# Lead-in of an attention block with a gated Mish layer: one row turned on TensorE, eight maxima moved behind the first step

## The chip, the cores and the metric

One core of a Trainium2 chip. The metric is device time in microseconds of one execution, the median of three runs. Engines: PE (TensorE) multiplies, PEld is its weight load, DVE is VectorE, ACT ScalarE, POOL GpSimd, SP SyncE, which here only issues DMAs. All matrices are 32-bit floats.

## The reference

```python
xn = layernorm(x)                       # x: 2048 x 512
q, k, v = xn @ wq, xn @ wk, xn @ wv     # 32 query heads of 16, one key and one value head of 16
p = softmax(q_h @ k.T / 4)              # per head, 2048 x 2048
s = concat_h(p @ v) @ wo
g = silu(mish(xn @ w1 + b1) @ w2)       # 1792 hidden columns
return x + s * g
```

## The kernel before, in words

Queries come in 4 chunks of 512 rows. With 32 heads that makes 128 head-chunk pairs; four of them are a **unit** `v` (32 units), held in a tile `qt` of 128 partitions: two halves `a` of 64 partitions, and two column planes `p`. Per half a query has 16 high rows, 16 high rows again, 16 low rows and, in rows 48 and 49, its negated row maximum in two parts; `ks` holds the keys' high and low parts with ones below, so that one matmul over 64 rows gives the score less the maximum.

A **step** is one block of 128 keys for one unit; there are 512. In a step TensorE computes four score tiles **E** (line 1056), ScalarE takes their exponentials into `pt` (line 1058), and two steps later eight **PV** matmuls (line 1143) add value-weighted sums, a column of ones giving the softmax's divisor. The maxima of a unit must be known before its first E: for each 128 queries and 512 keys, TensorE computes a score tile **M** (line 1078) and VectorE reduces it to a maximum (line 1082). A unit has 64 such maxima, four in each step on average, worked about a unit ahead (`LEAD = 20` steps). What is left of TensorE goes to **X**, the projections `xps` (query, Mish and output layers), of which a chunk of up to eight stands in each step: the function `waves` pairs a half matmul of X on 64 rows of the array with an E or M on the other 64. A large X group ends with its bank being copied out.

Ahead of step 0 is the **lead-in**. There x is normalized, transposed (line 303) and projected to keys and values in four chunks (line 341, bank `kp`). ScalarE writes the keys' high part (line 346) and copies the value part (line 355), VectorE writes the low part (line 238); TensorE turns the values (line 360) and VectorE copies them into `vaug` (line 363). The four use the same bank `kp`/`vp`, so a chunk's projection follows the copy of the chunk before. Lead-in work is ordered by a small planner: each task has an engine, an estimated duration, the tasks it depends on, and a priority; at each turn the earliest is written out. Maxima are not tasks: `m_ready` says when the next pair (one of each half, both halves side by side) can go, in the order `MSEQ`, by the arrival of query rows (`qready`), of the key chunk (`kready`) and by free PSUM banks (three for M). X is filled in where TensorE would be idle. A list written by the planner fixes the order of each engine's instructions; the hardware then only waits.

The first unit's query rows are split by ScalarE (high, line 703) and VectorE (low) and moved by DMAs on SP's queue (line 721). When 68 maxima are there, all 64 of unit 0 among them, `c_rows` reduces them on VectorE to a row (lines 1104 to 1109), turns it in blocks of 32x32 (line 1114), and eight DMAs put the blocks into rows 48 and 49 of `qt` (line 1122). Maxima of unit 1 go on. The lead-in ends when the planner holds the row for moved and each half has `2 * LEAD` = 40 maxima, 80 in all; step 0 follows, with four maxima in each step from then on. In later units the row is made in the same way.

Of the kernel before, what the change touches and what calls it, by code (L numbers as in the profile page):

```python
# [32 lines left out]
NU = 8 * NC  # L33
LEAD = 20
NWARM = 24
E0 = 74
# [90 lines left out]
def block_kernel(ctx: ExitStack, tc: tile.TileContext, x, wq, wk, wv, wo, w1, b1, w2, out):  # L127
# [234 lines left out]
    def v_out(c):  # L362
        dve.tensor_copy(vaug[:, 4 * c:4 * c + 4, 0:DH], vp_of[c][:, :, 16:32])

# [330 lines left out]
    def q_group(c, b):  # L695
        it = item("wq", ("q", b), wq[:, P * b:P * (b + 1)].rearrange("(t p) n -> p t n", p=P))

        def post(ps):
# [12 lines left out]
            for k in range(2):  # L711
                v = 8 * c + 2 * b + k

                def dmas(v=v, k=k, parts=((0, 0), (0, 1), (1, 0), (1, 1))):
                    q = qt_of[v] = qts[v % 3]
                    for p, a in parts:
                        o = 64 * a
                        r = 64 * k + 16 * (2 * p + a)
                        for d, src in ((o, qh), (o + 16, qh), (o + 32, ql)):
                            sp_at(0.63)  # L720
                            sp.dma_start(f(q[d:d + 16, p]), f(src[r:r + 16]))  # L721
                if first:
                    lead["qdma"](lambda ps, dmas=dmas: dmas(parts=[(p, a) for p in ps for a in range(2)]))
                else:
                    for n in range(4):
                        at(16 * v - LEAD - 9 + 2 * n, lambda dmas=dmas, n=n: dmas(parts=(divmod(n, 2),)))

# [361 lines left out]

    def m_sides(h, n):  # L1090

        ahead = m_next[h] - m_next[1 - h]
        lo = max((4 - MLAG - ahead + 1) // 2, 4 - (32 * NU - m_next[1 - h]))
        hi = min((4 + MLAG - ahead) // 2, 32 * NU - m_next[h])
        return max(min(n, hi), lo)

    def c_rows(v):

        mp = sb.tile([P, 2, 3, 8], F32R, tag="mp", name=f"mp{v}", bufs=2)
        mx = f(mp[:, :, 0])  # L1100
# [15 lines left out]
        def move():  # L1116
            q, cr = qt_of[v], w["cr"]
            for a in range(1, -1, -1):
                r = 64 * a + 48
                for b in range(4):  # L1120
                    sp_at(0.68)
                    sp.dma_start(f(q[r:r + 2]).rearrange("o p (t b n) -> b o (p t) n", b=4, n=32)[b],
                                 cr[32 * b + 16 * a:32 * b + 16 * a + 16])
        return reduce, parts, turn, move

# [157 lines left out]

    def q_low(fn):
        lead["qlow"] = task("DVE", 0.69, fn, at=T["ACT"] + 0.7)

    def q_dma(fn):
        v = len(qready)
        qready[v] = None

        def move(p):
            fn(ps=(p,))
            qready[v] = (qready[v] or ()) + (now[0] + 6 * 0.63 + 2.0,)
        for p in range(2):
            task("SP", 6 * 0.63, lambda p=p: move(p), [lead["qlow"]], prio=1 + p + 2 * v)

# [25 lines left out]
    for c in range(A_LO // 4, NC):  # L1322
        sums = [task("ACT", 0.8, lambda t=t: stats_a(t, 0), at=xat[t], prio=2.8) for t in range(4 * c, 4 * c + 4)]
        means = task("ACT", 0.22, lambda c=c: means_a(slice(4 * c, 4 * c + 4)), sums, prio=2.8)
        st += [task("ACT", 0.8, lambda t=t: stats_a(t, 1), [means], prio=2.8) for t in range(4 * c, 4 * c + 4)]
    kv_done = None
    for c0, c1 in ((0, 1), (1, 2), (2, 3), (3, 4)):
        z = slice(4 * c0, 4 * c1)
# [8 lines left out]
        for c in range(c0, c1):  # L1337
# [47 lines left out]
            vc = task("ACT", 0.59, lambda c=c: v_copy(c), [kp], lat=0.7)  # L1385
            bank("v", 1, k0, [kl, vc])
            vtr = task("PE", 0.5, lambda c=c: v_transpose(c), [vc])
            vo = task("DVE", 0.22, lambda c=c: v_out(c), [vtr])
            bank("v", 1, vtr, [vo])

# [5 lines left out]
    def m_ready(t):  # L1396
        if min(m_next) >= 2 * LEAD or rows and rows[-1].end is None:
            return None
# [5 lines left out]
    def best(eng):  # L1404
        found = None
        for k in plan[eng]:
            s = k.start(T[eng])
            if s is not None:
                rank = max(s, T[eng] + 0.1) + WAIT_US * k.prio
                if found is None or rank < found[2]:  # L1410
                    found = (s, k, rank)
        return found

    begun = [0]
# [4 lines left out]
    while True:  # L1419
# [12 lines left out]
        if m is not None and b and b[0] < T["PE"] + 0.2 and T["DVE"] > T["PE"] + 1.0 and not twin[0]:  # L1432
            m = None
        if m is not None and (b is None or m <= b[0] + 0.05 or T["DVE"] < T["PE"] + 0.3 and m <= T["PE"] + 0.1):
            opts.append((m, "PE", "M"))
        elif b:
            opts.append((b[0], "PE", b[1]))
# [6 lines left out]
        s, e, k = min(opts, key=lambda o: o[0])  # L1444
        if cdone[0] is not None and s >= cdone[0] - 0.4 and min(m_next) >= 2 * LEAD:
            break
# [3 lines left out]
        if k == "M":  # L1450
# [8 lines left out]
            if vdone[0] == 0 and min(m_next) >= m_need(0):  # L1459
                vdone[0] = 1  # L1460
                r = c_rows(0)
                r1 = task("DVE", 0.85, lambda r=r: (r[0](), r[1](), r[2]()), prio=-4)
                rows[:] = [r1]

                def move():
                    r[3]()
                    cdone[0] = now[0] + 2 * 0.65 + 2.0
                task("SP", 2.6, move, [r1])
        elif k == "X":
# [54 lines left out]
    for s in range(NS + 2000):  # L1524
        inm = s < NS - LEAD
        if inm or cur["chunk"]:
# [4 lines left out]
            def em(k):  # L1531
                n = m_sides(1 - h, k // 2) if inm else 0
                x = deque(lambda i=i: e_one(s, i) for i in range(4))
                y = deque(lambda: m_one(1 - h) for _ in range(n))
                r = [[], []]
                for op in EM:
                    if op == "M" and y:
                        r[1 - h].append(y.popleft())
                    elif op == "E":
                        r[1 - h].append(x.popleft())  # L1540
                r[h] = [lambda: m_one(h) for _ in range(4 - n if inm else 0)]
                return r
# [78 lines left out]
```

## Time and profile before

| | us |
|---|---|
| median of three runs | 1575.3 |
| lowest, highest | 1575.14, 1575.66 |
| the profiled execution | 1576.14 |
| its span, first to last instruction | 1574.4 |
| TensorE, VectorE, ScalarE, GpSimd busy in the span | 1559.6, 1351.8, 1301.9, 642.4 |

The granted TensorE clock is 1.00, the upper of its two levels, in every slice of the span. Times in the profile count from the span's start. A matmul's recorded duration includes its way through the array, and successive ones overlap: the distance of two starts, not the duration, says what one costs in a row.

### The profile page before, as it was taken

The numbers are of one execution on the slowest core, as the hardware profiler recorded it, in microseconds if no ns is written. First come the engines' busy times: TensorE is split into PE (matmuls) and PEld (weight loads), VectorE is DVE, ScalarE is ACT, GpSimd is POOL, SyncE is SP. The second block draws the span as 40 slices with busy tenths as digits, with TensorE's granted clock in tenths as the row PEclk, the third lists the DMA queues.
The fourth block names the chain that finished last, engine by engine and source line by source line (L and its number), as shares of the span: only waits on it lengthen the run. The fifth ranks groups of instructions, "written<-read, shape, count | busy, mean of one in ns | idle before, by whom it ended". The sixth has DMA issues, their size and how long they took to land.

```text
span 1574.4 us, 32018 instructions
## 1 busy us (share of the span) xinstructions
PE 1559.6 (99%) x11910; PEld 845.4 (54%) x11910; DVE 1351.8 (86%) x2307; ACT 1301.9 (83%) x2502; POOL 642.4 (41%) x667
## 2 busy tenths in 40 slices
PE   8999999999999999999999999999999999999998
PEld 5455555555555555555555555555555555555555
DVE  7898888888989888888998988889889998888852
ACT  6488888798998878878888787887898879788876
POOL 4677376175474203604425042260342415225222
PEclk9999999999999999999999999999999999999999
DMA  6223232132331314122031411221423222031110
GB/s 196 94 84 118 58 98 103 56 127 85 116 98 47 110 25 137 51 73 77 26 101 52 125 58 45 85 69 43 140 59 105 61 93 64 19 111 32 48 44 29
DMA packets 75082, 124.45 MB, mean 79 GB/s; under 512 B 21744, under 2 KB 36336, under 8 KB 74928
## 3 DMA queue, kind: packets, MB, share of 16 engines
q1 hardware_dynamic: 74784, 122.29, 24.9%
q8 instruction: 94, 1.54, 0.4%
q14 instruction: 60, 0.49, 0.1%
q10 hardware_dynamic: 144, 0.13, 0.0%
HBM read 74.65 MB, written 26.21 MB: 64 GB/s over the span
## 4 chain that ended last, share of the span: by engine, by line
PE 95%; ACT 1%; DVE 1%; DMA 1%; POOL 1%; SPq 1%; issue 0%; DVEq 0%; ACTq 0%
PE xps L120 45%; PE pv L1143 32%; PE e L1056 7%; PE m L1078 7%; PE pv L1136 1%; PE xps L116 1%; DVE mb L1082 1%; PE e L1029 1%; PE tail L120 0%; DMA rawws<-in_dram 0%; PE tailx L120 0%; DMA xin<-in_dram 0%; PE kp L341 0%; ACT xin L211 0%; SPq L721 0%
## 5 line engine op out<-in xcount | busy, mean ns | idle before, releaser
L1082 DVE TENSOR_REDUCE mb<-m 128x1 f32<-128x512 f32 x2048 | 1273.0, 682 | 171.2 <-PE m L1078 146.5
L1058 ACT ACTIVATE pt<-e 128x512 f32<-128x512 f32 x1978 | 1038.2, 601 | 214.4 <-PE e L1056 211.3
L1078 PE MATMUL m<-ks,qt 48*128 48x512 f32 (+1 forms) x2048 | 842.1, 420 | 1.0 <-DVE mb L1082 0.7
L1056 PE MATMUL e<-qt,ks 64*128 64x512 f32 x1978 | 722.6, 398 | 0.3 <-ACT pt L1058 0.3
L1143 PE MATMUL pv<-pt,vaug 128*32 128x512 f32 x3968 | 528.4, 605 | 0.0
L1078 PEld LDWEIGHTS m<-ks,qt 48*128 48x128 f32 (+1 forms) x2048 | 371.6, 185 | 56.2 <-DVE mb L1082 20.3
L1056 PEld LDWEIGHTS e<-qt,ks 64*128 64x128 f32 x1978 | 367.0, 186 | 5.3 <-ACT pt L1058 0.7
L120 PE MATMUL xps<-xt,ws 64*128 64x512 f32 x1224 | 339.0, 409 | 0.0
L120 PE MATMUL xps<-wbs,act 64*128 64x512 f32 x1248 | 336.9, 406 | 0.1
L120 PEld LDWEIGHTS xps<-xt,ws 64*128 64x128 f32 x1224 | 210.7, 185 | 198.7 <-ACT pt L1058 129.1
L120 PEld LDWEIGHTS xps<-wbs,act 64*128 64x128 f32 x1248 | 217.4, 185 | 173.3 <-ACT pt L1058 109.2
L174 POOL TENSOR_SCALAR t<-t 128x512 f32<-128x512 f32 x56 | 34.5, 616 | 327.7 <-ACT t L771 327.4
L1143 PEld LDWEIGHTS pv<-pt,vaug 128*32 128x32 f32 x3968 | 78.0, 108 | 132.4 <-issue 124.0
L164 POOL TENSOR_TENSOR hb<-hb,t 128x512 f32<-128x512 f32 x56 | 72.4, 1292 | 100.1 <-ACT t L784 76.2
L120 PE MATMUL xps<-xt,wq 64*128 64x512 f32 x336 | 93.1, 409 | 0.0
L120 PEld LDWEIGHTS xps<-xt,wq 64*128 64x128 f32 x336 | 57.9, 185 | 54.2 <-ACT pt L1058 34.4
L120 PE MATMUL xps<-wbs,ot_all 64*128 64x512 f32 x288 | 79.5, 408 | 0.0
L120 PEld LDWEIGHTS xps<-wbs,ot_all 64*128 64x128 f32 x288 | 49.5, 184 | 46.4 <-ACT pt L1058 29.3
L164 POOL TENSOR_TENSOR hb<-hb,u 128x512 f32<-128x512 f32 x56 | 72.3, 1292 | 4.4
L164 POOL TENSOR_TENSOR act<-hb,act 128x512 fp32r<-128x512 f32 x56 | 72.1, 1288 | 4.7
L164 POOL TENSOR_TENSOR u<-u,t 128x512 f32<-128x512 f32 x56 | 71.9, 1284 | 4.7
L164 POOL TENSOR_TENSOR oc<-oc,sc 128x512 f32<-128x512 f32 x16 | 20.7, 1293 | 122.4 <-ACT sc L1170 72.2
(160 smaller groups left out, 967.4 us busy)
## 6 DMA issues: line engine op xcount, KB each, us to landing
wbs<-w SPq DMA_DIRECT2D x36, 512.0 KB
ws<-w SPq DMA_DIRECT2D x35, 512.0 KB
qt<-qh SPq DMA_DIRECT2D x256, 32.0 KB
w<-wbs SPq DMA_DIRECT2D x14, 512.0 KB
w<-ws SPq DMA_DIRECT2D x14, 512.0 KB
wq<-wq SPq DMA_DIRECT2D x13, 512.0 KB
wbs<-wo SPq DMA_DIRECT2D x11, 512.0 KB
rawws<-in_dram SPq DMA_DIRECT2D x21, 256.0 KB
```

The costliest lines, as they stand in the source:

```text
L116: self.pe.matmul(ps, self.lhs(), self.rhs(), start=(self.k == 0), stop=(self.k == self.tot - 1))
L120: i = self.pe.matmul(ps, self.lhs()[o], self.rhs()[o], start=(self.k == 0 and self.halves == 0), stop=(self.k == self.tot - 1 and self.hal ...
L164: eng.tensor_tensor(out=o, in0=a, in1=b, op=op)
L174: pool.tensor_scalar(o, o, lim, 0.0, op0=ALU.min, op1=ALU.max)
L1029: pe.matmul(es[a][:, C // 2 * m:C // 2 * (m + 1)], ks[o:o + 64, P * (k + m):P * (k + m + 1)], q[o:o + 64, i // 2, z], start=True, stop=True)
L1056: pe.matmul(e, ks[o:o + 64, P * k:P * (k + 1)], q[o:o + 64, p], start=True, stop=True)
L1058: r = act.activation(pt, e, AF.Exp, scale=0.25)
L1078: pe.matmul(m, q[o, p, P * t:P * (t + 1)], ks[o, C * kb:C * (kb + 1)], start=True, stop=True)
L1082: r = dve.reduce_max(out=mb_of[v][:, kb, z:z + 1], in_=m, axis=AX.X)
L1136: pe.matmul(o[32 * j:32 * j + 32, z], vaug[:, k + m], pts[j][:, C // 2 * m:C // 2 * (m + 1)], start=(k + m == 0), stop=(k + m == 15))
L1143: pe.matmul(o[32 * j:32 * j + 32], vaug[:, k], pt, start=(k == 0), stop=(k == 15))
```

## The change

- The value copy out of PSUM is done by ScalarE (`v_out`).
- In the lead-in the row of unit 0 is turned by TensorE into a PSUM bank, copied out by ScalarE and moved with two DMAs (`turn_pe`, `wide`, `move_wide`); for that the tile `mp` keeps its parts in another order there. Later units are turned as before.
- Query rows: the DMAs of the first unit's high rows are written out ahead of those of the low rows, and the planner lets them start after the high part instead of after the low part.
- A pair of maxima is not written out if VectorE would then end later than 1.3 us after a key chunk's projection whose low part is still to come (`low_due`).
- The lead-in ends with 36 maxima in each half, 72 in all (`FIRST`). From then on every second step takes six maxima in place of four, as long as the total stays within what it was before: steps 0, 2, 4 and 6, if all go in.

```diff
+FIRST = 36
+MORE = 2
     def v_out(c):
-        dve.tensor_copy(vaug[:, 4 * c:4 * c + 4, 0:DH], vp_of[c][:, :, 16:32])
+        act.activation(vaug[:, 4 * c:4 * c + 4, 0:DH], vp_of[c][:, :, 16:32], AF.Copy)
...
-                    for p, a in parts:
-                        o = 64 * a
-                        r = 64 * k + 16 * (2 * p + a)
-                        for d, src in ((o, qh), (o + 16, qh), (o + 32, ql)):
+                    for d, src in ((0, qh), (16, qh), (32, ql)):
+                        for p, a in parts:
+                            o = 64 * a + d
+                            r = 64 * k + 16 * (2 * p + a)
                             sp_at(0.63)
-                            sp.dma_start(f(q[d:d + 16, p]), f(src[r:r + 16]))
+                            sp.dma_start(f(q[o:o + 16, p]), f(src[r:r + 16]))
...
+        def turn_pe():
+            w["ps"] = ps_v.tile([P, C], F32, tag="v", name="crp")[0:32, 0:P]
+            pe.transpose(w["ps"], f(mt)[:, 16:48], ident)
+
+        def wide():
+            w["cr"] = sb.tile([P, P], F32, tag="y0", name="crw", bufs=1)[0:32]
+            act.activation(w["cr"], w["ps"], AF.Copy)
+
+        def move_wide():
+            q = f(qt_of[v]).rearrange("(a r) p (t n) -> r a (p t) n", a=2, n=P)
+            for o in range(2):
+                sp_at(0.68)
+                sp.dma_start(q[48 + o], w["cr"][16 * o:16 * o + 16])
+        if lead:
+            return reduce, parts, turn_pe, wide, move_wide
...
     def q_low(fn):
+        lead["qhigh"] = T["ACT"] + 0.8
         lead["qlow"] = task("DVE", 0.69, fn, at=T["ACT"] + 0.7)
...
-            task("SP", 6 * 0.63, lambda p=p: move(p), [lead["qlow"]], prio=1 + p + 2 * v)
+            task("SP", 6 * 0.63, lambda p=p: move(p), at=lead["qhigh"], prio=1 + p + 2 * v)
...
-            vo = task("DVE", 0.22, lambda c=c: v_out(c), [vtr])
+            vo = task("ACT", 0.25, lambda c=c: v_out(c), [vtr])
...
-        if min(m_next) >= 2 * LEAD or rows and rows[-1].end is None:
+        if min(m_next) >= FIRST or rows and rows[-1].end is None:
...
+    def low_due():
+
+        own = [kp.end + 0.8 for kp, kl in lows if kl.end is None and kp.end is not None]
+        return min(own, default=10.0 ** 6)
...
+        if m is not None and max(T["DVE"], m + 0.45) + 1.2 > low_due() + 0.5:
+            m = None
...
-                r1 = task("DVE", 0.85, lambda r=r: (r[0](), r[1](), r[2]()), prio=-4)
+                r1 = task("DVE", 0.65, lambda r=r: (r[0](), r[1]()), prio=-4)
+                r2 = task("PE", 0.15, r[2], [r1], prio=-4)
+                r3 = task("ACT", 0.35, r[3], [r2], prio=-4)
+                bank("v", 1, r2, [r3])
                 rows[:] = [r1]
 
                 def move():
-                    r[3]()
-                    cdone[0] = now[0] + 2 * 0.65 + 2.0
-                task("SP", 2.6, move, [r1])
+                    r[4]()
+                    cdone[0] = now[0] + 2.4
+                task("SP", 1.3, move, [r3])
...
             def em(k):
-                n = m_sides(1 - h, k // 2) if inm else 0
+                tot = 6 if s % MORE == 0 and sum(m_next) + 6 <= 4 * (LEAD + s + 1) else 4
+                n = m_sides(1 - h, (k + tot - 4) // 2, tot) if inm else 0
...
-                r[h] = [lambda: m_one(h) for _ in range(4 - n if inm else 0)]
+                r[h] = [lambda: m_one(h) for _ in range(tot - n if inm else 0)]
```

## Rows read from the trace of the kernel before

**Rows 1.** The page, parts 1 and 4: busy time by engine, and the chain by engine.

```profile
PE 1559.6 (99%) x11910; PEld 845.4 (54%) x11910; DVE 1351.8 (86%) x2307; ACT 1301.9 (83%) x2502; POOL 642.4 (41%) x667
...
PE 95%; ACT 1%; DVE 1%; DMA 1%; POOL 1%; SPq 1%; issue 0%; DVEq 0%; ACTq 0%
```

**Rows 2.** Windows: stretch, length, busy us of PE, PEld, DVE, ACT, POOL, clock, DMA.

```profile
25.00:74.45 49.45, 45.30 (x192) 23.50 (x190) 44.76 (x79) 27.84 (x64) 27.50 (x37) 1.00 0.36 118
80.00:88.04 8.04, 7.01 (x42) 4.06 (x43) 8.04 (x14) 6.14 (x12) 3.05 (x3) 1.00 0.37 104
111.00:411.00 300.00, 300.00 (x2322) 160.39 (x2314) 264.18 (x450) 256.21 (x490) 166.04 (x171) 1.00 0.28 89
1537.00:1574.40 37.40, 31.91 (x337) 19.23 (x329) 10.45 (x22) 23.08 (x46) 10.18 (x8) 1.00 0.08 29
```

**Rows 3.** Timeline of VectorE, 37 to 66 us: start, length, what, [idle before it <-releaser].

```profile
37.72 2.66 DVE L1082 TENSOR_REDUCE mb<-m 128x1 f32<-128x512 f32 x4 [0.59 <-PE m L1078]
...
48.97 0.73 DVE L238 SCALAR_TENSOR_TENSOR ks<-ks,ksgn,kp 112x512 fp32r<-112x512 f32 x1
50.65 1.29 DVE L1082 TENSOR_REDUCE mb<-m 128x1 f32<-128x512 f32 x2 [0.94 <-PE m L1078]
...
56.51 4.87 DVE L1082 TENSOR_REDUCE mb<-m 128x1 f32<-128x512 f32 x8 [0.86 <-PE m L1078]
61.30 0.73 DVE L238 SCALAR_TENSOR_TENSOR ks<-ks,ksgn,kp 112x512 fp32r<-112x512 f32 x1
63.54 2.48 DVE L1082 TENSOR_REDUCE mb<-m 128x1 f32<-128x512 f32 x4 [1.50 <-PE m L1078]
```

**Rows 4.** Timeline of ScalarE, 17 to 60 us.

```profile
17.55 0.60 ACT L703 ACTIVATE qh<-xps 128x512 fp32r<-128x512 f32 x1 [1.31 <-PE xps L116]
...
46.41 0.59 ACT L355 ACTIVATE vt<-kp 32x512 f32<-32x512 f32 x1
...
51.32 0.70 ACT L327 ACTIVATE xf<-xp 128x256 f32<-128x256 f32 x2
...
58.50 0.59 ACT L355 ACTIVATE vt<-kp 32x512 f32<-32x512 f32 x1
```

**Rows 5.** The tile vp: operation, count, duration in ns (min/median/max).

```profile
L360 PE MATMUL vp<-ident,vt x16: 220/222/245, 23.2 to 63.9; 32*128 32x32 f32 x16
L363 DVE COPY vaug<-vp x4: 204/212/216, 23.9 to 65.9; 128x64 f32<-128x64 f32 x4
```

**Rows 6.** Timeline of VectorE, 74 to 90 us.

```profile
74.24 0.21 DVE L1114 STREAM_TRANSPOSE cr<-mp 128x32 f32<-128x32 f32 x1
...
77.29 12.05 DVE L1082 TENSOR_REDUCE mb<-m 128x1 f32<-128x512 f32 x20 [0.47 <-PE m L1078]
```

**Rows 7.** Timeline of TensorE, 79 to 92 us.

```profile
79.94 0.46 PE L120 MATMUL xps<-xt,wbs 64*128 64x512 f32 x1 [0.21 <-POOL hb L164]
...
88.04 1.06 PE L1143 MATMUL pv<-pt,vaug 128*32 128x512 f32 x8
...
89.37 0.39 PE L120 MATMUL xps<-xt,wbs 64*128 64x512 f32 x1
...
89.60 0.39 PE L120 MATMUL xps<-xt,wbs 64*128 64x512 f32 x1
...
90.89 1.07 PE L1143 MATMUL pv<-pt,vaug 128*32 128x512 f32 x8
```

**Rows 8.** Timeline of SP, which issues DMAs, 18 to 80 us.

```profile
18.18 1.23 SPq L721 DMA_DIRECT2D qt<-qh  x2
...
74.52 5.34 SPq L1122 DMA_DIRECT2D qt<-cr  x8
```

**Rows 9.** The chain that ended last, in order of time, after 1500 us.

```profile
1532.38 1.75 DMA oc<-os
...
1568.88 0.70 DVE y L164
```

**Rows 10.** Windows of line 116 alone (projections in the lead-in): stretch, length, PE, PEld.

```profile
58.30:79.10 20.80, 13.51 (x48) 8.32 (x48) 1.00 0.05 13
```

More of the change, by code (lines that the diff above doesn't have):

```diff
@@ L1088, in m_one, with m_sides @@
         held[0].append(top)
-    def m_sides(h, n):
+    def m_sides(h, n, tot=4):
         ahead = m_next[h] - m_next[1 - h]
-        lo = max((4 - MLAG - ahead + 1) // 2, 4 - (32 * NU - m_next[1 - h]))
-        hi = min((4 + MLAG - ahead) // 2, 32 * NU - m_next[h])
+        lo = max((tot - MLAG - ahead + 1) // 2, tot - (32 * NU - m_next[1 - h]))
+        hi = min((tot + MLAG - ahead) // 2, 32 * NU - m_next[h])
         return max(min(n, hi), lo)
     def c_rows(v):
-        mp = sb.tile([P, 2, 3, 8], F32R, tag="mp", name=f"mp{v}", bufs=2)
+        mt = sb.tile([P, 48], F32R, tag="mp", name=f"mp{v}", bufs=2)
+        mp = mt.rearrange("p (s a z) -> p a s z" if lead else "p (a s z) -> p a s z", a=2, s=3)
         mx = f(mp[:, :, 0])
@@ L1326, in block_kernel @@
     kv_done = None
+    lows, norms = [], []
     for c0, c1 in ((0, 1), (1, 2), (2, 3), (3, 4)):
@@ L1386, in block_kernel @@
             bank("v", 1, k0, [kl, vc])
+            lows.append((kp, kl))
             vtr = task("PE", 0.5, lambda c=c: v_transpose(c), [vc])
-            vo = task("DVE", 0.22, lambda c=c: v_out(c), [vtr])
+            vo = task("ACT", 0.25, lambda c=c: v_out(c), [vtr])
             bank("v", 1, vtr, [vo])
@@ L1444, in block_kernel @@
         s, e, k = min(opts, key=lambda o: o[0])
-        if cdone[0] is not None and s >= cdone[0] - 0.4 and min(m_next) >= 2 * LEAD:
+        if cdone[0] is not None and s >= cdone[0] - 0.4 and min(m_next) >= FIRST:
             break
```

## The prediction

> **What bounds the kernel now.** I read the page first. TensorE is busy for 99% of the span, and the chain that ended last runs through TensorE for 95% [rows 1]. The windows then tell stages apart [rows 2]: from 111 to 411 us TensorE is never idle, while VectorE (264 of 300 us) and ScalarE (256) have slack. In the lead-in, 25 to 74.45 us, it is the other way: VectorE is busy for 44.8 of 49.5 us, and TensorE has 4.2 us of recorded idle time and many short, separate matmuls besides. The eight microseconds from 80 to 88 are the first three steps, with VectorE busy for all 8.04. So the lead-in and these steps go at VectorE's pace, all that follows at TensorE's.
>
> For the reader this has one consequence. From 88 us on a microsecond is won only where TensorE gets less to do. A step that begins sooner wins its whole lead, less the TensorE work that the shorter lead-in no longer did.
>
> The VectorE queue shows where the lead-in loses time [rows 3]. Between two runs of maxima stands the low part of a key chunk (line 238), and after two of the three in this stretch VectorE waits for TensorE: 0.94 us at 50.65 and 1.50 us at 63.54; after the other, at 37.72, 0.59 us; and 0.86 us at 56.51, while TensorE projects keys. That is 3.9 us. The low part could have come earlier: ScalarE had read the chunk's bank for the last time at 47.00 and 59.09 [rows 4], yet VectorE came to it at 48.97 and 61.30, behind maxima queued before it.
>
> **The change, part by part.** Gains are negative.
>
> *Value copies to ScalarE.* A copy costs VectorE 0.212 us [rows 5]; the first lies ahead of the first maximum, so three count: 0.64 us off the bounding engine. ScalarE has no row of this form. Two 128x256 copies out of PSUM take it 0.70 us [rows 4], so 0.35 is the upper end for a 128x64 one and VectorE's own 0.21 the lower; I take 0.25 us four times. ScalarE is idle for 21.6 us of the stretch [rows 2], which hides it; without that cover the next chunk's copies are late by 0.25 us each.
>
> *The row turned by TensorE.* Off VectorE goes the turning, 0.21 us [rows 6]. With the copies: **-0.85 us**. TensorE gets one turning, between the 0.22 us of a 32x32 one [rows 5] and a full matmul's 0.39 us [rows 7]: I take 0.25, and 0.25 for ScalarE's copy out. What is queued behind it on TensorE are projections and maxima; were VectorE late with the row, they would wait too, by up to the 1.5 us of the longest wait in [rows 3], and I take nothing, since TensorE follows VectorE there anyway. SP issues two DMAs in place of eight that took 5.34 us [rows 8], 0.67 us each, so 1.3 us; the DMAs behind them on that queue, the next query rows among them, are free to go 4 us sooner, which nothing near waits for.
>
> The row shows VectorE turning in 0.21 us what TensorE and ScalarE need some 0.5 us for. The Trainium skill ("VectorE: DVE Perf Modes", "Rules for kernel authors") says that for 32x32 blocks VectorE's transpose is the fastest, which speaks against this part; its section "The three transpose paths" adds that VectorE can't cross 32-partition blocks, and the eight DMAs of this trace fit that. By the rule alone this part would be a loss of 0.3 us; with the queue's rows it is a gain.
>
> *From the row to the first step.* Now the row is done on VectorE at 74.45, and the first step begins at 79.94 [rows 6, 7], 5.5 us later, since twelve maxima (7.2 us at 0.60 us apart: 12.05 us for 20 in [rows 6]) are put into the lead-in after the row. Afterwards there are four (2.4 us), and the row decides: 0.25 + 0.25 + 1.3 us, a landing of 1.75 us as of another small transfer between on-chip tiles [rows 9], and 0.15 us of handing over make 3.7 us to the first E. The planner can open the step before the row lands (its first slots hold no E); I take 3.0 us, so **-2.5 us** (-1.7 if the step waits for the landing, -3.1 if the four maxima alone decide).
>
> *Key parts first.* A pair of maxima is held back when it would end later than about 1.3 us after the chunk's projection. VectorE then waits in front of the key part rather than behind it, about 0.5 us each time, and has maxima in stock after it. Of the 3.9 us I take **-1.5 us**; the ends are -3.9 (all closed) and +0.5 (each wait only changes its place, and one grows).
>
> *High rows in front.* The first DMA leaves at 18.18 us [rows 8], when ScalarE has just written the high part (17.55 + 0.60 [rows 4]); so it does now, and SP goes on without a pause, since VectorE's low part is there before its turn. Cost and gain 0; the bounds are -0.5 and +0.3 us, a DMA issue either way.
>
> *First three steps.* They take 8.1 us now (79.94 to 88.04 [rows 7]), of which VectorE is never free. Until the first PV VectorE has 24 maxima to do after the row now and 20 then, but the steps themselves hold 16 in place of 12: 9.6 us, less what stays in the three banks at the first PV, as now. With no backlog at the start I take 8.8 us, **+0.7 us** (0 to +2.4, four maxima in full). The first PV thus comes 4.15 us sooner.
>
> *Steps 3 to 6.* Four more maxima: two matmuls go side by side in 0.23 us (89.37 to 89.60 [rows 7]), 0.116 us each: **+0.46 us** on TensorE. VectorE's 20 maxima take 12.1 us, TensorE's four steps 11.9 (2.85 us each, from one PV to the next in [rows 7], and this 0.46): they nearly tie, and I allow up to +1.0.
>
> *Projections not done.* Between 58.3 and 79.1 us TensorE did 48 projection matmuls beside the maxima, 2.3 in a microsecond [rows 10]. What the lead-in loses behind the keys, about 2.5 us, leaves 5.8 of them to steps that TensorE fills, at 0.23 us each: **+1.3 us** (0 if idle time of TensorE takes them up; +2.6 if the whole 4.9 us by which the first step comes sooner count).
>
> Sum: -0.85 - 1.5 - 2.5 + 0.7 + 0.46 + 1.3 = -2.4 us. The profiled execution took 1576.14 us, its span 1574.4; the median is 0.84 below the former. 1576.14 - 2.4 - 0.84 = **1572.9 us**.
>
> **The rivals.** About 0.2% (3.15 us) is what a measurement of this kernel can tell from no change: faster is below 1572.15, slower above 1578.45.
>
> *All of the idle time goes.* For it: after the keys are in, VectorE would have stock in every gap. Against it: one gap (0.86 us) lies in TensorE's key projections, which stay. With -3.9 for the gaps and +0.4 for projections the sum is -5.7: 1569.6 us.
>
> *Nothing is gained.* The waits move ahead of the key parts (+0.5), the first step waits for the row (-1.7), and the deferred maxima come back in the first steps for the most part (+1.6, and +0.46 after them), all with no projection lost: with -0.85 the sum is 0.0 and the time 1575.3 us. For it: VectorE is busy in all of 80 to 88. This is also where the rule of the Trainium skill above would lead, the turning bringing nothing because maxima and not the row decide.
>
> *Slower.* If 12 or more projection matmuls are put off, a whole group moves past its place, and the last one misses the slots among the last heads. It runs alone: 12 matmuls at 0.23 us are 2.8 us more of TensorE than now, then as much again in which nothing stands beside it, and its evacuation of 0.7 us [rows 9] follows. With none of the gaps closed: -0.85 - 2.5 + 0.7 + 0.46 + 2.8 + 2.8 + 0.7 = +4.1, 1579.4 us. For it: TensorE is idle for only 5.5 us of the last 37.4 [rows 2], so little of it would be hidden. Against it: a deferral of 12 is twice what I find.
>
> **How the numbers follow.** My forecast has 0.46, all idle time gone 0.26, nothing gained 0.17, slower 0.11. Of the forecast's own spread (1571.0 to 1574.5) a third lies below 1572.15: faster 0.26 + 0.15 = 0.41. Slower is 0.11 and a little of the no-gain case, 0.13; the same 0.46. The range reaches from just under the first rival, 1569.4, to a little above no gain, 1576.2; the slow case and a tail of the fast one are left out.
>
> **What would show it.** Right: no VectorE copy or turning before the first step; key parts some 2 us sooner after their projection and no wait of a microsecond behind them; the turning (74.24 now) over 2 us sooner, the first step 3 us after the row, first PV near 84 us; 8 maxima more in the first seven steps; steady stage and end unchanged. Wrong: a wait of E for the row's DMAs over a microsecond; first PV sooner by over 6 us or under 2; a stretch after 1507 us that is longer than now; TensorE idle in steps 3 to 8.

## The result and the profile after

The changed kernel takes 1580.7 us (median of 7 runs, 1579.2 to 1582.15) against 1575.42 us before on the same chip (7 runs, 1575.14 to 1575.93): ratio 1.0033, 95% interval 1.0024 to 1.0043. It is slower, by 5.3 us. The profiled execution took 1581.7 us, its span 1579.9.

The page of the changed kernel, parts 1 and 4, answers to [rows 1]:

```profile
PE 1564.2 (99%) x11907; PEld 848.6 (54%) x11907; DVE 1352.2 (86%) x2302; ACT 1301.7 (82%) x2506; POOL 642.2 (41%) x668
...
PE 95%; DVE 2%; ACT 1%; POOL 1%; DMA 0%; issue 0%; SPq 0%; DVEq 0%; ACTq 0%; POOLq 0%
```

The bound is the same, TensorE, and it is busy for 4.6 us longer with three matmuls fewer. The windows tell where (columns as in [rows 2]; the eighth number is the granted clock):

```profile
46.00:51.00 5.00, 2.80 (x16) 1.45 (x16) 4.65 (x8) 3.96 (x8) 2.58 (x6) 0.94 0.18 52
51.00:57.00 6.00, 5.99 (x21) 4.52 (x22) 3.37 (x6) 2.94 (x8) 1.85 (x3) 0.50 0.00 0
...
67.00:71.00 4.00, 4.00 (x11) 2.16 (x10) 3.57 (x7) 0.00 (x0) 3.84 (x4) 0.57 0.00 0
...
76.36:83.22 6.86, 5.23 (x25) 3.50 (x25) 2.39 (x4) 2.56 (x5) 5.78 (x7) 1.00 0.13 34
83.22:91.78 8.56, 7.81 (x43) 3.74 (x39) 8.34 (x14) 6.70 (x12) 3.28 (x4) 1.00 0.23 72
111.00:411.00 300.00, 300.00 (x2324) 160.94 (x2322) 263.92 (x450) 256.56 (x492) 171.99 (x177) 1.00 0.29 91
1542.57:1579.90 37.33, 31.80 (x333) 19.18 (x325) 10.46 (x22) 22.96 (x46) 10.17 (x8) 1.00 0.08 29
```

The steady stage and the end are as before: 300.00 of 300 us, and in the last 37.3 us 31.80 us busy against 31.91. The first line is a stretch in which TensorE worked for 2.80 of 5 us. Towards its end, at 50.4 us, the granted clock falls to 0.50, the lower level (1.2 of 2.4 GHz), and stays there for 6.8 us; from 67.5 to 70.9 us it is at 0.50 a second time. In the kernel before it is 1.00 in every slice, and the first stretch is fuller:

```profile
46.00:51.00 5.00, 4.24 (x29) 2.91 (x27) 4.05 (x8) 4.96 (x12) 2.98 (x3) 1.00 0.19 54
```

Next the last key chunk's first transposition and the first steps, on TensorE in the changed kernel:

```profile
49.64 0.63 PE L305 MATMUL xp<-ident,xin 128*128 128x128 f32 x4 [0.80 <-DVE mb L1084]
...
77.15 0.27 PE L1129 MATMUL crp<-ident,mp 128*32 128x128 f32 x1
78.18 2.97 PE L118 MATMUL xps<-xt,wbs 128*128 128x512 f32 x12 [0.76 <-ACT crw L1133]
82.02 0.93 PE L118 MATMUL xps<-xt,wbs 128*128 128x512 f32 x3 [0.87 <-POOL u L166]
82.88 0.49 PE L122 MATMUL xps<-xt,wbs 64*128 64x512 f32 x1
...
91.78 1.06 PE L1161 MATMUL pv<-pt,vaug 128*32 128x512 f32 x8
...
94.67 1.06 PE L1161 MATMUL pv<-pt,vaug 128*32 128x512 f32 x8
...
97.17 1.51 PE L1080 MATMUL m<-ks,qt 64*128 64x512 f32 x3
98.62 1.07 PE L1161 MATMUL pv<-pt,vaug 128*32 128x512 f32 x8
101.48 1.06 PE L1161 MATMUL pv<-pt,vaug 128*32 128x512 f32 x8
```

and on VectorE, the counterparts of [rows 3, 6]:

```profile
46.35 0.75 DVE L240 SCALAR_TENSOR_TENSOR ks<-ks,ksgn,kp 112x512 fp32r<-112x512 f32 x1 [0.76 <-PE m L1080]
...
53.74 2.48 DVE L1084 TENSOR_REDUCE mb<-m 128x1 f32<-128x512 f32 x4 [1.86 <-PE m L1080]
...
64.12 0.75 DVE L240 SCALAR_TENSOR_TENSOR ks<-ks,ksgn,kp 112x512 fp32r<-112x512 f32 x1 [0.98 <-ACT vt L357]
...
83.44 9.66 DVE L1084 TENSOR_REDUCE mb<-m 128x1 f32<-128x512 f32 x16 [4.69 <-PE m L1080]
93.35 2.56 DVE L1084 TENSOR_REDUCE mb<-m 128x1 f32<-128x512 f32 x4 [0.25 <-PE xps L122]
96.24 3.68 DVE L1084 TENSOR_REDUCE mb<-m 128x1 f32<-128x512 f32 x6 [0.33 <-PE xps L122]
```

The reader is to see three things. Of the key parts in this stretch the second comes sooner (46.35 against 48.97) and the third, that of the last key chunk, later (64.12 against 61.30). VectorE, relieved of eight maxima between the row and the first step, stands idle there for 4.69 us. And from one PV to the next it is 2.89 us, then 3.95, then 2.86: a step with six maxima lasts 1.1 us longer than one with four. VectorE's six reductions take 3.68 us, and three of the six M matmuls stand last before the PV.

The account, by the milestones of the two traces: the row's parts are ready 2.15 us later (76.36 against 74.21), from there to the first E 0.8 us is lost (6.86 against 6.07), from the first E to the first PV 0.8 (8.56 against 7.76), in the next nine steps 2.3 (tenth PV at 119.67 against 113.66), and 0.4 us comes back after that: 5.6 us of span. These are single executions. The profile of e5 below, whose instructions up to the first E are those of the kernel before in the same order, has the row's parts ready at 73.44, the first E at 79.53 and the first PV at 87.27, each about 0.8 us sooner. So where a milestone stands scatters by that much, while the distances agree (6.09 and 7.74 us there, 6.07 and 7.76 before).

### The profile page after: what moved, and what is told of

Same layout as the page of the kernel before. It is cut to its first block, busy times and chain, and to the rows that moved or that the text cites. A ratio compares the mean times of both kernels' runs of the same rounds, so it can differ in the third digit from the quotient of the medians.

```text
span 1579.9 us, 32001 instructions
## 1 busy us (share of the span) xinstructions
PE 1564.2 (99%) x11907; PEld 848.6 (54%) x11907; DVE 1352.2 (86%) x2302; ACT 1301.7 (82%) x2506; POOL 642.2 (41%) x668
## 4 chain that ended last, share of the span: by engine, by line
PE 95%; DVE 2%; ACT 1%; POOL 1%; DMA 0%; issue 0%; SPq 0%; DVEq 0%; ACTq 0%; POOLq 0%
PE xps L122 43%; PE pv L1161 31%; PE e L1058 9%; PE m L1080 7%; DVE mb L1084 1%; PE kp L343 1%; PE xps L118 1%; PE pv L1154 1%; PE e L1031 1%; PE tail L122 0%; PE tailx L122 0%; PE xp L305 0%; DMA xin<-in_dram 0%; ACT pt L1035 0%; PE tail L1249 0%
```

## The experiments

All kernels compute the whole output; where work is added, it is named. Milestones are those of each kernel's profile. Differences are of medians, against the kernel before on the same chip (1576.12, 1576.21, 1575.76 and 1576.26 us for the groups e, f, g with e5, and h).

| | row ready | first E | first PV | tenth PV | last M to end | median | ratio [95%] |
|---|---|---|---|---|---|---|---|
| before | 74.21 | 80.28 | 88.04 | 113.66 | 68.5 | | |
| after | 76.36 | 83.22 | 91.78 | 119.67 | 68.7 | +5.3 | 1.0033 [1.0024, 1.0043] |
| e1 no deferral | 76.49 | 82.14 | 90.33 | 115.97 | 71.3 | +5.5 | 1.0033 [1.0022, 1.0045] |
| e2 deferral alone | 73.44 | 80.16 | 89.03 | 118.13 | 68.6 | +4.2 | 1.0030 [1.0018, 1.0042] |
| e3 no hold | 72.42 | 76.96 | 85.54 | 113.33 | 71.4 | +4.1 | 1.0025 [1.0015, 1.0035] |
| e4 TensorE kept busy | 73.92 | 80.04 | 88.61 | 116.47 | 68.7 | +3.5 | 1.0023 [1.0013, 1.0032] |
| f1 turning, copies | 74.63 | 80.66 | 88.51 | 114.17 | 68.8 | +2.1 | 1.0011 [1.0002, 1.0020] |
| f2 f1 + deferral | 76.12 | 82.18 | 90.75 | 118.58 | 68.8 | +4.8 | 1.0029 [1.0020, 1.0038] |
| f3 turning alone | 74.14 | 80.37 | 88.11 | 113.76 | 68.8 | +0.1 | 0.9999 [0.9991, 1.0008] |
| f4 f1 + fives | 73.62 | 79.67 | 87.64 | 115.69 | 68.8 | +4.1 | 1.0025 [1.0015, 1.0035] |
| g2 f1 + hold | 74.37 | 80.69 | 87.82 | 113.53 | 68.7 | -0.9 | 0.9997 [0.9988, 1.0006] |
| g4 69 X, no hold | 72.75 | 83.37 | 89.62 | 115.39 | 68.8 | +2.6 | 1.0016 [1.0008, 1.0025] |
| g5 69 X, hold | 72.21 | 81.40 | 87.65 | 113.40 | 68.9 | +2.3 | 1.0015 [1.0006, 1.0023] |
| h1 turning, early rows | 73.37 | 80.63 | 87.20 | 112.83 | 68.7 | -0.9 | 0.9995 [0.9986, 1.0003] |
| h2 after, late rows | 73.20 | 78.45 | 87.03 | 114.70 | 71.4 | +4.3 | 1.0030 [1.0019, 1.0042] |
| h3 after, VectorE copies | 73.14 | 78.37 | 86.92 | 114.70 | 68.7 | +1.5 | 1.0012 [1.0003, 1.0022] |

**The deferral, taken out and alone.** e1 is the changed kernel with 80 maxima before the first step and four in each; e2 is the kernel before with the deferral and nothing else.

```diff
-FIRST = 36
+FIRST = 40
...
-                tot = 6 if s % MORE == 0 and sum(m_next) + 6 <= 4 * (LEAD + s + 1) else 4
+                tot = 4
```

> The changed kernel with all 80 maxima in the lead-in and four in every step (its tail needs two fence instructions, since one projection group more is left for the end). Theory A (a step with six maxima waits for VectorE: 3.95 us against 2.85): the seventh PV comes 17.2 us after the first, as before the change, not 19.3; VectorE has no 4.7 us gap ahead of the first step. Theory B (the lead-in is late because TensorE runs thin and its clock falls to half): the row is still ready near 76.4 us and the clock mean still below 1. Together: first PV near 90 to 91 us, time 1578 to 1580 us, of which the tail's extra group is 2 to 3. If neither holds, PV distances stay at 19.3.

> The kernel before with the deferral alone (72 maxima in the lead-in, six in steps 0, 2, 4, 6). Theory A: seventh PV 19.3 us after the first, against 17.2; the first PV itself at 87 to 88 us, so 1576.5 to 1577.5 us. Rival (a deferred maximum costs TensorE's 0.116 us alone, as predicted): 17.7 us between the PVs, first PV 2 us sooner, 1574 us. The clock stays at 1.00 in both.

The deferral alone makes the kernel 4.2 us slower. Its first E comes 0.12 us sooner, and even that is less than the 0.77 us by which the row's parts were ready sooner (as they were in e5, with nothing changed ahead of them). A window of e2 and a line of its VectorE timeline show why:

```profile
73.44:80.16 6.72, 4.98 (x22) 3.52 (x23) 2.58 (x6) 3.25 (x5) 6.15 (x7) 1.00 0.02 2
```

```profile
80.38 1.29 DVE L1084 TENSOR_REDUCE mb<-m 128x1 f32<-128x512 f32 x2 [4.33 <-PE m L1080]
```

Between the row and the first E TensorE is busy for 4.98 of 6.72 us; the same stretch of the kernel before has 4.99 of 6.07 us:

```profile
74.21:80.28 6.07, 4.99 (x24) 3.06 (x25) 5.57 (x10) 3.26 (x5) 5.51 (x7) 1.00 0.02 2
```

The planner filled the place of the maxima with projections (80 of them begin before the first E, 74 in the kernel before), so the stretch did not become shorter; the maxima that filled VectorE's free time there now stand in steps that they lengthen. But not all of the 4.2 us are the deferral's. I had expected a clock of 1.00, and e2's falls at 88.2 us, for 3.4 us:

```profile
83.00:88.00 5.00, 4.50 (x22) 2.02 (x21) 5.00 (x9) 4.15 (x8) 0.00 (x0) 1.00 0.10 23
88.00:92.00 4.00, 3.90 (x19) 1.41 (x19) 2.29 (x5) 1.99 (x5) 1.47 (x3) 0.57 0.00 0
```

Its first two PVs lie 4.28 us apart in place of 2.85, and all six of its runs have a mean clock under 1.000. What the deferral costs at full clock is read from f1, f2 and f4 below. e1 shows the same from the other side: without the deferral the tenth PV comes 3.7 us sooner than in the changed kernel. But its first steps began with 71 projections done, its last projections among the steps come 3.03 us after the last M (0.24 us before it in the kernel before), and from the last M to the end it takes 71.3 us, 2.8 more. Part of that is an addition of mine: a small matmul and a copy of six columns after each pair of groups in the tail of e1, e3 and h2 keep the two halves of a bank in order. There are two such places in e1, and they begin 0.76 and 0.42 us ahead of what follows them, so up to 1.2 of the 2.8 us are theirs. Both times, 1581.6 us for e1 and 1580.3 for e2, lie above what I had expected.

**The hold.** e3 leaves it out:

```diff
-        if m is not None and max(T["DVE"], m + 0.45) + 1.2 > low_due() + 0.5:
-            m = None
```

> The changed kernel without the rule that holds maxima back for the key part (tail with fences, as in the run without deferral). Theory B: TensorE isn't thin at 46 to 51 us, the clock stays at 1.00, the row is ready at 73 to 74.5 us in place of 76.4; with a tail group more 1577 to 1579 us. Rival (the value copies on ScalarE and the order of GpSimd's work make chunk 3 late, not the rule): row at 76 us or later, as in the changed kernel.

The first E comes at 76.96, 3.3 us sooner than before, with the row ready at 72.42 and only 68 projections done. The granted clock stays at 1.00 in the profile, as theory B has it. The steps with six maxima take back 2.2 us by the tenth PV, and the tail, with projections left over and matmuls added as in e1, 2.9 us; so the time, 1580.3 us, is above the range.

**TensorE kept busy.** e4 is the changed kernel with ten matmuls whose result nobody reads, in two fives ahead of the last key chunk's first two transpositions.

```diff
+        if t in (12, 13) and cur["g"] is None:
+            fillb = ps_x.tile([P, C], F32, tag="x", name="busy")
+            for _ in range(5):
+                pe.matmul(fillb, qts[2][:, 0, 0:P], qts[2][:, 0], start=True, stop=True)
```

> The changed kernel with ten needless matmuls ahead of the transposes of two blocks of the last chunk, where TensorE is thin (about 2.2 us of work at full clock into a free bank). Theory B in its clock form: granted clock 1.00 from 50 to 57 us, chunk 3's key projection over 2 us sooner, row ready at 73.5 to 75 us, 1577.5 to 1579 us. Rival (the clock is a consequence, the chunk is late through GpSimd and ScalarE): clock 1.00 yet the row stays within 0.7 us of 76.4, and the time within 0.7 us of the changed kernel's.

The windows of e4:

```profile
46.00:51.00 5.00, 4.32 (x23) 2.92 (x24) 4.58 (x8) 3.65 (x7) 2.81 (x8) 1.00 0.18 52
51.00:57.00 6.00, 6.00 (x32) 3.94 (x31) 4.31 (x8) 4.02 (x11) 1.97 (x3) 1.00 0.14 56
```

With useless work in it TensorE does more useful work afterwards: of the 32 matmuls in 51 to 57 us four are useless, which leaves 28 against 21 in the changed kernel. The granted clock stays at 1.00 throughout, in the second stretch too, the row is ready 2.4 us sooner, the first PV comes 3.2 us sooner. So the 2 us of the row's delay are TensorE's clock after a thin stretch. (The planner has a filler of its own, the matmul `warm`, where it expects TensorE idle: two at 48.38 us in the kernel before, one at 45.53 in the changed kernel, none in the waits that end at 49.64 and 51.02.) The times differ by less than the profiles (3.5 us above before in place of 5.3), since the changed kernel's own runs spread: the four of 7 with a mean clock of 0.996 or 0.997 have spans of 1578.9 to 1580.4, the three with 0.999 1577.4 to 1578.0. These three stand where e4's ten runs stand (1576.8 to 1578.7). Of the 5.3 us some 2 are thus the clock's, and some 3 remain in e4, of which the steps with six hold 2.2 by the tenth PV.

**Turning and value copies.** f3 keeps the turning on TensorE (and the order of the query DMAs) alone, f1 adds the value copies on ScalarE; both have 80 maxima, no hold, and query rows that wait for their low rows. f2 is f1 with the deferral, f4 f1 with eight steps of five:

```diff
-                tot = 6 if s % MORE == 0 and sum(m_next) + 6 <= 4 * (LEAD + s + 1) else 4
+                tot = 5 if sum(m_next) + 5 <= 4 * (LEAD + s + 1) else 4
```

> The first run of this group with the value copies back on VectorE: what is left of the change is the row's turning on TensorE and ScalarE with two DMAs, and the order of the query DMAs. Theory A: the four copies took 0.2 us each of VectorE, so this is 0.2 to 0.9 us above the first run and still 0 to 2 us below before. Rival B: the turning is what costs, 0.5 us or more above before. Rival D: neither copies nor turning matter, and the planner's order alone does; then this run and the first differ by an amount that no 0.2 us copy explains (over 1.2 us).

> The changed kernel without the hold for the low key parts, without the earlier start of the high query rows, and with 80 maxima before the first step and four in each (what is left: the row turned by TensorE and ScalarE, two row DMAs, value copies by ScalarE, the new order of the query DMAs). Theory A: the loss comes from the deferred maxima (about 3.7 us by the tenth PV) and from the hold (third key chunk late), so with both gone the kernel is 0.5 to 2.5 us faster than before: first E 0.5 to 2 us earlier than 80.28, PVs 2.85 us apart from the first, no granted clock under 1.00 between 44 and 78 us, seven projection groups in the tail and about 11 us from the last PV to the end. Rival B: the new path of the row (TensorE queue, ScalarE queue, DMA) is itself longer than VectorE's turning and eight DMAs; then the stretch from the row to the first E is 6 us or more as in the changed kernel, and the time is 0.5 us or more above before.

> As the run beside it (row turned by TensorE, value copies by ScalarE), but with 72 maxima before the first step and six in every other step until 8 are made up. Theory A: VectorE waits for the row's way to the first E anyway, so leaving out 8 maxima there frees nothing, and each step with six costs 1.1 us: 3 to 4.5 us more than the run beside it. Rival C: the first E comes earlier by what the 8 maxima took (8 x 0.61 us), which pays for the longer steps: within 0.7 us of the run beside it.

> As the second run of this group, with five maxima in each of the first eight steps instead of six in every other one. Theory A: a step with five holds VectorE 5 x 0.61 = 3.0 us against the 2.85 of a step and fits better into three M banks: 0.1 to 0.3 us a step, so 0.8 to 2.4 us above the first run and 1.5 us or more below the second. Rival E: what costs is the number of deferred maxima, whatever their spread: within 0.7 us of the second.

The turning alone brings nothing: +0.1 us. Yet it does what it says. SP's timeline and the window from the row to the first E, in f3:

```profile
76.53 1.22 SPq L1139 DMA_DIRECT2D qt<-crw  x2
```

```profile
74.14:80.37 6.23, 5.15 (x25) 3.07 (x26) 5.39 (x11) 3.52 (x6) 5.63 (x7) 1.00 0.07 15
```

The last row DMA is issued by 77.75, against 79.86 before (74.52 + 5.34, [rows 8]). But TensorE has 5.15 us of work in the 6.23 us, which it does in its written order ahead of the first E, and the first E follows it without a recorded wait. The row was not what the first E waited for.

The copies, added to the turning, cost 2 us, which no copy of 0.2 us explains (rival D), and again it is the clock. The windows of f1:

```profile
45.00:49.00 4.00, 1.99 (x16) 1.31 (x13) 4.00 (x7) 2.49 (x6) 1.32 (x2) 1.00 0.29 87
49.00:53.00 4.00, 4.00 (x19) 2.56 (x17) 1.23 (x3) 3.04 (x8) 0.46 (x1) 0.57 0.00 0
```

and of f4:

```profile
45.00:49.00 4.00, 1.99 (x13) 1.31 (x12) 4.00 (x8) 2.72 (x5) 1.76 (x2) 1.00 0.37 108
49.00:53.00 4.00, 4.00 (x26) 2.63 (x26) 2.31 (x5) 3.77 (x11) 0.57 (x1) 1.00 0.02 4
```

f1, f2 and f4 give TensorE the same instructions in the same order up to the turning of the row, and in 45 to 49 us f1 and f4 are equally thin, 1.99 of 4 us. Yet in f4's profile the clock stays at 1.00, in f1's it is at 0.50 for 3.4 us, and in f2's for 6.8 us (48.1 to 54.9). The row's parts are ready at 73.62, 74.63 and 76.12, in that order. So one order runs with or without the fall. f1's eleven runs bear it out: the two with a mean clock of 1.000 have spans of 1574.5 and 1575.2, the five with 0.999 1574.3 to 1576.5, the four with 0.998 1577.3 to 1577.9, while all of f3's lie between 1574.3 and 1575.0. By the two runs at full clock the copies cost nothing. (The stretch of 6 us or more that rival B asks for is there in f1, 6.03 us, but so it is before, 6.07, and in f3, 6.23.)

The deferral on top costs 2.7 us more in f2, and the same between the runs with a mean clock of 1.000 (1577.6, 1577.6 and 1578.2 in f2): this is its price without the clock. Five at a time is hardly cheaper (rival E): the PVs of f4 stand 3.33 us apart,

```profile
87.64 1.07 PE L1161 MATMUL pv<-pt,vaug 128*32 128x512 f32 x8
90.99 1.06 PE L1161 MATMUL pv<-pt,vaug 128*32 128x512 f32 x8
94.32 1.07 PE L1161 MATMUL pv<-pt,vaug 128*32 128x512 f32 x8
```

0.48 us above a step with four, where a step with six has 1.1. Each maximum beyond four costs about half a microsecond, whatever the spread.

**Steps with six and with two.** e5 is the kernel before with uneven steps and the same count:

```diff
+                tot = (4 + 2, 4, 4 - 2, 4)[s % 4] if 16 <= s < 416 else 4
```

> The kernel of before with 6, 4, 2 and 4 maxima in turn in the 400 steps from the 17th, so that 100 steps have six and 100 have two, and the count is the same. Theory A: a step with six is held by VectorE (3.93 us against 2.85 in the trace of the changed kernel), a step with two is held by TensorE and gives back at most 0.25 us: 80 to 110 us above before. Rival: TensorE sets the steps and VectorE evens out over two steps: within 10 us of before. Second rival: VectorE sets all steps, and a step with two gives back what one with six took: within 15 us.

It takes 1710.29 us, 134.5 above before, 1.34 for each pair of a six and a two, more than any of the three theories said. TensorE's PVs and VectorE's maxima in the first round of e5:

```profile
124.25 1.07 PE L1145 MATMUL pv<-pt,vaug 128*32 128x512 f32 x8
128.19 1.06 PE L1145 MATMUL pv<-pt,vaug 128*32 128x512 f32 x8
131.05 1.07 PE L1145 MATMUL pv<-pt,vaug 128*32 128x512 f32 x8
133.89 1.06 PE L1145 MATMUL pv<-pt,vaug 128*32 128x512 f32 x8
136.82 1.06 PE L1145 MATMUL pv<-pt,vaug 128*32 128x512 f32 x8
```

```profile
125.81 3.68 DVE L1084 TENSOR_REDUCE mb<-m 128x1 f32<-128x512 f32 x6 [0.35 <-PE m L1080]
129.75 2.48 DVE L1084 TENSOR_REDUCE mb<-m 128x1 f32<-128x512 f32 x4 [0.26 <-PE m L1080]
132.61 1.29 DVE L1084 TENSOR_REDUCE mb<-m 128x1 f32<-128x512 f32 x2 [0.38 <-PE m L1080]
135.54 2.48 DVE L1084 TENSOR_REDUCE mb<-m 128x1 f32<-128x512 f32 x4 [1.64 <-PE m L1080]
```

The steps with six, four, two and four last 3.94, 2.86, 2.84 and 2.93 us. The step with two is no shorter than one with four, since TensorE's other work fills it (busy for all of its 2.84 us), and VectorE then idles for 1.64 us. The step with six is VectorE's. Neither engine evens out over two steps. This round costs 1.2 us more than four even steps; why the mean over all rounds is 1.34 was not followed up.

**The hold without the deferral, and projections forced in.** g2 is f1 with the hold; I expected the loss there.

> The changed kernel with 80 maxima before the first step and four in each, and with the query rows waiting for their low rows as before; the hold for the low key parts is kept (it is the run with turning and value copies alone, and the hold). Theory A: the hold keeps maxima off VectorE and TensorE ahead of a key part, TensorE is thin at 46 to 50 us, its granted clock falls, and the third chunk's keys come later: 0.7 to 3 us above the run without the hold, that is 1579 to 1581. Rival: the hold costs nothing and it was the start of the high query rows that cost: within 0.7 us of the run without the hold (1578.3).

My theory fell, and so did the rival, a time like f1's: g2 is 0.9 us below before, within what can be told from no change, and 3.0 us below f1 (each against its own before), with the row ready at 74.37 and the clock at 1.00 (TensorE busy for 4.61 of the 5 us from 46). Beside the turning and the copies the hold costs nothing. g4 and g5 let the first step begin only after 69 projections (g4 without the hold, g5 with the hold, early query rows and the copies on VectorE):

```diff
+                xdone[0] += 3
...
-        if cdone[0] is not None and s >= cdone[0] - 0.4 and min(m_next) >= FIRST:
+        if cdone[0] is not None and s >= cdone[0] - 0.4 and min(m_next) >= FIRST and xdone[0] >= 69:
```

> The changed kernel without the hold and without deferred maxima, and with at least 69 projection matmuls ahead of the first step (the run without the hold had 66 there and began its first step 3.3 us sooner than before, with one projection group more in the tail). Theory A: three matmuls more (0.8 us) bring the tail back to seven groups, so most of the 3.3 us stays: first E at 78 to 79.5, steps 2.85 us apart from the first PV, about 11 us from the last PV to the end, 1 to 2.5 us below before. Rival F: the matmuls left out ahead of the first step and those in the tail are the same work, and what starts the kernel sooner is only work put off: 0.3 us below before or slower.

> The changed kernel without deferred maxima, with the value copies on VectorE as before, and with at least 69 projection matmuls ahead of the first step; hold and early query rows are kept. Six projection groups are left in the tail. Theory A: the six groups give up to 3 us, the hold costs 1 to 3 us through the late third key chunk: 1574 to 1577.5. Rival F: as in the run beside it, what is done early is not done late and the sum stays: within 1 us of 1576.2 whatever the tail.

My theories missed both times; g4 came out slower, as its rival had it, g5 as neither had it. The edit did more than these expectations say: its counter leaves out the first twelve projections, and in the traces 83 begin before the first E, 9 more than before and 15 more than in e3. Three more were not tried. The tail is short again (68.8), but in g4 TensorE waits for what the last projections need:

```profile
80.79 2.31 PE L118 MATMUL xps<-xt,wbs 128*128 128x512 f32 x9 [0.87 <-ACT hb L765]
...
83.37 0.39 PE L122 MATMUL xps<-xt,wbs 64*128 64x512 f32 x1
```

The row was ready 1.5 us sooner than before and the first E came 3.1 us later. Projections left out are paid for in the tail (2.9 us in e3, up to 1.2 of it the added matmuls), projections forced in are paid for in front (3.1 us in g4): most or all of what a start 3.3 us sooner had won.

**Which part makes the thin stretch.** h2 and h3 are the whole change less one part each, h1 one part beside the turning:

```diff
 # h2: query rows wait for their low rows, as before
-            task("SP", 6 * 0.63, lambda p=p: move(p), at=lead["qhigh"], prio=1 + p + 2 * v)
+            task("SP", 6 * 0.63, lambda p=p: move(p), deps=[lead["qlow"]], prio=1 + p + 2 * v)
 # h3 (and h1): value copies on VectorE, as before
-            vo = task("ACT", 0.25, lambda c=c: v_out(c), [vtr])
+            vo = task("DVE", 0.22, lambda c=c: v_out(c), [vtr])
```

> Row turned by TensorE and the high query rows sent early; value copies on VectorE, no hold, four maxima in each step and 80 before the first. Theory G: early high query rows alone disturb the order of the lead-in (TensorE thin at 46 to 51 us, clock under 1.00, row's parts ready after 75.5): 1.5 us or more above the run with the turning alone, which stood at before. Rival H: the early rows do this only together with the copies on ScalarE and the hold: within 0.8 us of before, row's parts ready by 74.8.

> The whole change, but the high query rows wait for the low ones as before (eight projection groups are left in the tail, which cost about 2.7 us in the two runs that had them). Theory G: without the early rows TensorE stays busy at 46 to 51 us, the granted clock stays at 1.00 and the row's parts are ready at 74 to 75, as in the run with hold and copies; the deferral's 3.5 to 4.5 us by the tenth PV are left, so tenth PV at 117 to 118.5 and the end 6 to 7 us above before with the tail's. Rival H: it is the deferral's other target for the maxima that changes the order, and the row's parts come at 75.5 or later, the tenth PV at 119 or later.

> The whole change but for the value copies, which stay on VectorE (seven projection groups in the tail). Theory G: early query rows and hold are enough for the thin stretch: row's parts ready at 75.5 or later, tenth PV at 119 or later, 4 to 6 us above before. Rival I: the copies on ScalarE are needed for it: row's parts ready by 74.8, granted clock 1.00 throughout, tenth PV at 117 to 118.5 and 3 to 4.5 us above before, which is the deferral alone.

Early rows alone cost nothing (h1, -0.9 us). In the whole change, taking out either the early rows or ScalarE's copies is enough: the row is ready at 73.20 and 73.14, 3.2 us sooner than in the changed kernel, and the clock stays at 1.00; e3 shows the same for the hold. This holds for the profiled executions: h3's eleven runs have mean clocks from 0.995 to 1.000. The windows of h3:

```profile
46.00:51.00 5.00, 3.94 (x24) 2.20 (x23) 4.64 (x9) 4.81 (x11) 1.73 (x8) 1.00 0.19 53
51.00:57.00 6.00, 4.71 (x22) 2.48 (x23) 5.79 (x10) 4.20 (x9) 4.76 (x5) 1.00 0.36 145
73.14:78.37 5.23, 3.79 (x18) 2.69 (x18) 2.39 (x4) 2.04 (x4) 4.90 (x7) 1.00 0.09 22
```

Here the first E does come 1.9 us sooner than before and the first PV 1.1; the steps with six take back 2.2 by the tenth PV. h3 is 1.5 us above before, the changed kernel 5.3 (each against its own before); the 3.8 us between them are the clock and the other order of the lead-in together, and only e4 takes out the clock by itself. h2 ends 4.3 us above before, with a tail as long as e1's, though 77 projections had begun before its first E, as many as in the changed kernel. So that number alone does not decide the tail, and what does was not followed up.

No version was faster than the kernel before by more than its interval; h1 and g2 come nearest.

## Why the prediction was wrong

Forecast 1572.9, range 1569.4 to 1576.2; measured 1580.7. The premise that the lead-in goes at VectorE's pace did not follow from its own row: in 25 to 74.45 us TensorE was busy for 45.30 us, VectorE for 44.76 [rows 2]. The steps, in the order of the working:

- **Value copies and turning, -0.85.** The durations held: ScalarE's copy took 0.22 us and TensorE's turning 0.27, for 0.25 each. The gain did not. The turning alone gave +0.1 us, the copies on top of it +2.0 (f3, f1), and none in f1's runs with a mean clock of 1.000. The Trainium skill ("VectorE: DVE Perf Modes", "Rules for kernel authors") calls VectorE's transpose the fastest for 32x32 blocks. The trace agrees in the durations: 0.21 us on VectorE, 0.27 on TensorE and 0.27 on ScalarE in f3. By that rule the prediction had put a loss of 0.3 us, by the queue's rows a gain; f3's time shows neither.
- **From the row to the first step, -2.5.** This step failed. It took the twelve maxima after the row for what sets the stretch, and the row's DMAs for what would set it afterwards. Both stood beside TensorE, busy for 4.99 of the 6.07 us. It measured +0.8 in the change, +0.2 with the turning alone, +0.65 with the deferral alone, -0.85 in h3, and -1.5 in e3, the best, which had six projections fewer ahead of the first E. The idle time of TensorE in the stretch, 1.1 us, was the bound to look for as long as the projections stay. (The bound of -1.7, if the step waits for the landing, is -1.8 by its own terms, 3.7 less 5.5.)
- **Key parts first, -1.5.** The second key part did come 2.6 us sooner, but the third came 2.8 later, since its chunk's projection came five microseconds later (58.21 to 62.75 against 53.21 to 57.8). With the clock at 1.00, in e4, it begins at 56.27: 1.9 of the five are the clock's, the rest is the written order. The step looked at VectorE's waits and not at what TensorE would have left to do while VectorE held back; the bound of +0.5 had no room for a clock at 0.50. The hold alone is not to blame (g2), and the copies can bring the fall without it (f1).
- **High rows in front, 0.** Right by itself (h1), wrong in company (without it, in h2, the row is ready 3.2 us sooner than in the changed kernel).
- **First three steps, +0.7.** Right: from the first E to the first PV 0.8 us more.
- **Steps 3 to 6, +0.46.** The second step that failed. It compared sums over four steps, 12.1 us for VectorE and 11.9 for TensorE, as if work passed from one step to the next. Two steps with six cost 1.1 us each, 2.2 in all, and the steps between them gave nothing back (f4, e5).
- **Projections not done, +1.3.** Didn't occur in the change: 77 began before the first E, 74 before. A longer tail is real, 2.8 to 2.9 us in e3, e1 and h2 with up to 1.2 of it from the added matmuls; but these had 68, 71 and 77 begun, so the count that the step went by does not foretell it. That was the rival "slower", at 1579.4; the time came out near it by other ways.

The account of the two traces adds up by these: 2.15 for the row, 0.8 and 0.8 up to the first PV, 2.3 for the steps with six, less 0.4. Why the planner's order becomes thin with copies, early rows and hold together was not traced to a single decision. What the trace shows is that the last key chunk's first transposition begins at 49.64, behind four pairs' maxima, after a wait of 0.80 us for one of them; in h3, at 48.30.

## What to carry to other kernels

Before counting what leaves a stretch on one engine, look at what the others have to do in it: a shorter way for one row, or eight maxima fewer on VectorE, wins no more than TensorE's idle time there, unless work of TensorE goes too, and that work comes back elsewhere. Work spread over a loop has to fit each step, not the average of a few: in this kernel, with three banks between two engines (their number was not varied), a step with more is paid in full and a step with less gives nothing back. Where a planner writes the order, parts that are harmless in one company (the hold in g2, the early rows in h1) can make a thin stretch on TensorE in another, so the parts are to be measured together as well as alone. And where the granted clock falls in some executions only, kernels are to be compared at equal clock before a part is given its price.

## What was not expected of the hardware

The granted clock fell from 1.00 to 0.50 although TensorE was never idle for more than 0.80 us at a time: it worked for 2.80 of the 5 us around the fall. At 0.50 it got through 21 matmuls in six microseconds, at 1.00, in e4, through 28 of its own and four useless ones. The recorded busy time does not tell when the clock falls: f1's fell and f4's did not, each after 1.99 of 4 us and with the same order of instructions, and e2's fell after 4.50 of 5 us. f1 ran at mean clocks from 0.998 to 1.000, and its spans go from 1577.9 down to 1574.3.
